# Token loops staged with lags, one product spread over the barriers, and weight transposes in 128-row pieces, in a forward-and-backward transformer block

## The chip, the cores and the metric

The kernel runs on one core of one Trainium2 chip. The metric is the device time of one execution in microseconds (us); quoted times are medians over several executions. Engines are named as in the profile: PE is TensorE (matmul), PEld its weight loads, DVE is VectorE, ACT is ScalarE, POOL is GpSimd, SP is Sync, which here only issues transfers. "SPq" lines are Sync's transfer issues. "Hole" below means a stretch in which TensorE is idle.

## The reference

One block of linear attention followed by a SwiGLU feed-forward layer, each behind a LayerNorm, and all its gradients.

```python
def A(x, wqkv, wo):                       # 2048 tokens, D = 640, 32 heads of 20
    q, k, v = split_heads(x @ wqkv)
    phi = lambda t: where(t > 0, t + 1, exp(t)) + 1e-6
    pq, pk = phi(q), phi(k)
    kv, z = sum_tokens(pk * v), sum_tokens(pk)
    o = (pq @ kv) / (pq . z + 1e-6)
    return o @ wo
def B(x, w_gate, w_up, w_down):           # F = 1728
    return (silu(x @ w_gate) * (x @ w_up)) @ w_down
h  = x + A(layernorm(x), wqkv, wo)
h2 = h + B(layernorm(h), w_gate, w_up, w_down)
# outputs: h2, and the gradients of x, wqkv, wo, w_gate, w_up, w_down for a given grad_out
```

Everything is bfloat16. Token tiles have 128 rows, so there are 16 of them.

## The kernel before

The work is a line of stages with whole-token barriers between them. The names below are used throughout.

1. k/q loop: LayerNorm, transpose of the tile (`xnT`), products for k and q; then `z`.
2. `y`, `kvt`, `w2`: three small matrix products that make `W2`, while VectorE makes `pqs`.
3. a loop: `pqs @ W2`, second LayerNorm (`hn`, with `rstd` on GpSimd), transpose `hnT`.
4. `dm`: `grad_out @ w_down^T`, 32 steps of ten matmuls.
5. gate/up block, four times: `pg`, `pu`, VectorE's derivatives, transposes `stg`, then the weight gradients `dw`.
6. dhn/dp loop; 7. `gt`, `dkvt`, `wv2`, `dz`; 8. dk/dxn loop; 9. weight gradients `dwqk`, `dwo`, and the o loop with the output.

The parts that the change and the argument touch:

```python
for t in tiles:                                        # stage 1
    ... transposes of tile t on TensorE, copy of xnT on ScalarE ...
    for (dst, w0) in ((pk, D), (pqa, 0)):              # k and q of the SAME tile
        ps = mm("ps_kq"); mm_row(ps, xnT of tile t, wqk)
    if t % 4 == 3:
        nc.gpsimd.dma_start(out=scr_xn..., ...)        # also pk, pq and four of xnT
...
nc.gpsimd.dma_start(out=mat_v(scr_W2), in_=W2[:])      # stage 2: W2 stored plain
for t in range(ST + 1):                                # stage 3, hn one tile behind
    ...
for g in range(4):                                     # stage 4: all dm in one block
    for t in range(0, ST, 2):
        ... 10 matmuls; evacuation dme; nc.gpsimd.dma_start(out=scr_dm..., in_=dme)
...
W2T = mat("W2T")
nc.sync.dma_start_transpose(out=W2T[:], in_=scr_W2)    # stage 6: whole matrix
for t in range(ST + LAG):                              # dp two tiles behind dhn
    ...
nc.sync.dma_start_transpose(out=woT[:], in_=A_wo)      # whole matrices, also wqkvT, G, KV, Y, dKV
...
for t in range(ST + LAG):                              # stage 8
    nc.gpsimd.dma_start(out=xtv, in_=scr_xnT[t])       # loads of this tile, just in time
    nc.gpsimd.dma_start(out=pkr[:], in_=scr_pk_v[:, t, :])
    nc.sync.dma_start_transpose(out=pkT, in_=pkr[:])
    ...
```

A property of the program: a scheduler orders each engine's instructions at build time, by what it expects to be ready. So an instruction's place in a queue isn't its place in the source.

Of the kernel before, what the change touches and what calls it, by code (L numbers as in the profile page):

```python
# [9 lines left out]
BF16 = mybir.dt.bfloat16  # L10
# [4 lines left out]
P = 128  # L15
# [4 lines left out]
def kernel(  # L20
# [15 lines left out]
    LAG = 2  # L36
    GW = [448, 448, 448, 384]
# [53 lines left out]
    scr_W2 = dram.tile([D, D], BF16, name="scr_W2")  # L91
# [34 lines left out]
    def ln_rstd(mv, mean, rstd, t0, nt):  # L126
        v = small.tile([P, 4], FP32, name="lnv", tag="lnv")
        nc.gpsimd.tensor_scalar(out=v[:, :nt], in0=mv[:, :nt, 1], scalar1=1e-5, scalar2=None, op0=ALU.add)
        nc.gpsimd.tensor_tensor(out=rstd[:, t0:t0 + nt], in0=v[:, :nt], in1=nhalf[:, :nt], op=ALU.pow)
# [30 lines left out]
    dm0 = strips.tile([P, ST, GM], BF16, name="dm0", tag="S")  # L160
# [3 lines left out]
    for (t0, t1) in ((0, 1), (1, 2), (2, 4)):  # L164
        nc.sync.dma_start(out=x_tm[0][:, t0:t1, :], in_=x_v[:, t0:t1, :])
    for (c0, c1) in ((D, 2 * D), (0, D)):
        nc.scalar.dma_start(out=wqk[:, :, c0:c1], in_=A_wqkv[:, c0:c1].rearrange("(k p) n -> p k n", p=P))
    for (t0, t1) in ((4, 8), (8, 12), (12, 16)):
        nc.sync.dma_start(out=x_tm[t0 // 8][:, t0 % 8:(t1 - 1) % 8 + 1, :], in_=x_v[:, t0:t1, :])
# [25 lines left out]
    wvo = strips.tile([P, 2, DT, D], BF16, name="wvo", tag="S")  # L195
# [6 lines left out]
    pqa = big.tile([P, ST, D], BF16, name="pqa", tag="B")  # L202
    for (t0, t1) in ((0, 1), (1, 2), (2, 4), (4, 6), (6, 8), (8, 10), (10, 12), (12, 14), (14, 16)):
# [4 lines left out]
        for t in range(t0, t1):  # L208
# [6 lines left out]
            for (dst, w0) in ((pk, D), (pqa, 0)):  # L215
                ps = mm("ps_kq")
                mm_row(ps, lambda k: xnT[:, k, t * P:(t + 1) * P], lambda k, n0, n1: wqk[:, k, w0 + n0:w0 + n1], DT)
                e = fw("phi_e")
                r = fw("phi_r")
                nc.scalar.activation(out=e[:, :, :320], in_=row(ps), func=ACT.Exp)  # L220
                nc.scalar.activation(out=r[:, :, :320], in_=row(ps), func=ACT.Relu)
                nc.vector.tensor_scalar(out=e[:, :, :320], in0=e[:, :, :320], scalar1=1.0, scalar2=1e-6,
                                        op0=ALU.min, op1=ALU.add)
                nc.vector.tensor_tensor(out=half(dst[:, t, :]), in0=e[:, :, :320], in1=r[:, :, :320], op=ALU.add)
            if t % 4 == 3:
                sl = slice(t - 3, t + 1)
                nc.gpsimd.dma_start(out=scr_xn_v[:, sl, :], in_=xn[:, sl, :])
                nc.gpsimd.dma_start(out=scr_pk_v[:, sl, :], in_=pk[:, sl, :])
                nc.gpsimd.dma_start(out=scr_pq_v[:, sl, :], in_=pqa[:, sl, :])
                for tt in range(t - 3, t + 1):  # L230
                    nc.gpsimd.dma_start(out=scr_xnT[tt], in_=xnT[:, :, tt * P:(tt + 1) * P])
# [5 lines left out]
    nc.gpsimd.dma_start(out=wvo[:, 0], in_=A_wqkv[:, 2 * D:3 * D].rearrange("(k p) n -> p k n", p=P))  # L237
    nc.gpsimd.dma_start(out=wvo[:, 1], in_=A_wo.rearrange("(k p) n -> p k n", p=P))
# [6 lines left out]
    for i in range(DT):  # L245
# [3 lines left out]
        nc.scalar.copy(out=mask[:, i, :e1 - e0], in_=ps[:, 0, :e1 - e0])  # L249

# [22 lines left out]
    nc.gpsimd.dma_start(out=mat_v(scr_Yt), in_=Yt)  # L273
    for j in range(DT):
# [7 lines left out]
    W2 = big.tile([P, DT, D], BF16, name="W2", tag="B")  # L282
    for i in range(DT):
# [4 lines left out]
    nc.gpsimd.dma_start(out=mat_v(scr_W2), in_=W2[:])  # L288
# [4 lines left out]
    for t in range(ST + 1):  # L293
# [355 lines left out]
```

## Time and profile before

| | kernel before |
|---|---|
| time | 1001.98 us, median of 3 (1001.32 to 1008.93) |
| profiled execution | 1011.5 us, mean granted TensorE clock 0.958 |
| TensorE busy | 859.4 us, 85% |
| TensorE idle | 152 us; the prediction below sums it by stage |

How to read it: the page first gives each engine's busy time; then 40 slices of the span, a digit being the busy share in tenths. A timeline line has start, length, engine, source line, operation, output<-inputs, shapes, number of instructions, and in brackets the idle time just before the group and what ended it. The lines themselves are in the prediction below.

### The profile page before, as it was taken

To read this page: it belongs to the slowest core of one execution; us is meant where nothing else is said; L and a number is where in the kernel's file an instruction comes from. 1 tells how busy PE (TensorE), PEld (TensorE's weight loads), DVE (VectorE), ACT (ScalarE), POOL (GpSimd) and SP (SyncE) were. 2 spreads that over 40 slices of the span, in tenths; PEclk is the share of its full clock that TensorE was granted. 3 is DMA by queue.
4 is the path that set the end of the run, shared out by engine and by line. 5 is a ranking of instruction groups with operands and counts; after the bars stand their busy time and mean duration, and the time that the engine had idled before them with its cause. 6 is when DMAs were issued, how large, how long until landed. Compare 5 with 4: busy or idle time off the path is not lost.

```text
span 1011.5 us, 14023 instructions
## 1 busy us (share of the span) xinstructions
PE 859.4 (85%) x5461; PEld 533.6 (53%) x5461; DVE 425.0 (42%) x889; ACT 299.2 (30%) x421; POOL 253.1 (25%) x430
## 2 busy tenths in 40 slices
PE   2667956999999999999999199997948777997996
PEld 1445634555455455455567177775725454674663
DVE  6733988205705704804701067777113333400111
ACT  1666110447515514614501022222201222311100
POOL 5732136442232221231242001011101212113321
PEclk9999979999999999999999699998978999998998
DMA  9993598987995992982869935137798555699521
GB/s 285 153 282 117 123 237 203 212 210 182 208 285 110 231 276 65 216 221 49 205 204 210 111 103 187 33 116 229 173 204 189 121 124 134 106 242 290 147 79 39
DMA packets 277938, 174.82 MB, mean 173 GB/s; under 512 B 236032, under 2 KB 259264, under 8 KB 277872
## 3 DMA queue, kind: packets, MB, share of 16 engines
q1 hardware_dynamic: 251312, 79.36, 43.1%
q0 software_dynamic: 25248, 92.94, 29.8%
q10 hardware_dynamic: 1312, 1.64, 0.5%
q8 instruction: 42, 0.69, 0.3%
q14 instruction: 24, 0.20, 0.1%
HBM read 52.90 MB, written 64.01 MB: 116 GB/s over the span
## 4 chain that ended last, share of the span: by engine, by line
PE 54%; DVE 15%; DMA 13%; issue 6%; SPq 5%; ACT 3%; POOL 2%; POOLq 0%; DVEq 0%; ACTq 0%
PE ps_dw L400 16%; PE ps_dhn L117 10%; PE ps_dm L321 6%; PE ps_kq L117 5%; PE ps_dxn L550 3%; PE ps_o L599 3%; DMA ring<-pkr 2%; PE ps_dp L117 2%; DMA dh1T<-dh 2%; PE ps_gt L117 2%; SPq L592 2%; DMA xt<-scr_xnT 2%; PE pg L357 2%; DVE m_s L383 1%; DVE m_s L377 1%
## 5 line engine op out<-in xcount | busy, mean ns | idle before, releaser
L400 PE MATMUL ps_dw<-dd,hn 128*128 128x448 bf16 (+1 forms) x640 | 119.9, 346 | 7.0 <-DVE dd L382 6.9
L117 PE MATMUL ps_dhn<-wgT,cols 128*128 128x320 bf16 x864 | 120.8, 301 | 0.0
L117 PEld LDWEIGHTS <-cols 128*128 128x128 bf16 x864 | 85.1, 98 | 33.8
L400 PEld LDWEIGHTS <-hn 128*128 128x128 bf16 x640 | 62.6, 98 | 62.3 <-issue 8.7
L387 POOL DMA_DIRECT2D scr_dT<-stg x64 | 34.6, 541 | 171.5 <-DMA stg<-dd 153.2
L402 DVE CAST dwev<-ps_dw 128x896 bf16<-128x896 f32 (+3 forms) x12 | 10.9, 907 | 150.4 <-PE ps_dw L400 150.4
L117 PE MATMUL ps_kq<-wqk,xnT 128*128 128x320 bf16 x320 | 48.3, 308 | 26.2 <-ACT xnT L214 26.2
L550 PEld LDWEIGHTS <-ring 128*128 128x128 bf16 x480 | 49.6, 104 | 37.4 <-DMA ring<-dk 14.8
L599 PE MATMUL ps_o<-wd,mT 128*128 128x320 bf16 x448 | 67.7, 300 | 0.0
L550 PE MATMUL ps_dxn<-wqkvT,ring 128*128 128x320 bf16 x320 | 55.8, 318 | 13.8 <-DMA ring<-dk 13.8
L362 PE MATMUL pu<-wgu,hnT 128*128 128x448 bf16 (+1 forms) x320 | 63.6, 346 | 0.0
L357 PE MATMUL pg<-wgu,hnT 128*128 128x448 bf16 (+1 forms) x320 | 63.6, 346 | 0.0
L402 ACT CAST dwev<-ps_dw 128x896 bf16<-128x896 f32 (+1 forms) x20 | 17.6, 878 | 152.1 <-PE ps_dw L400 118.8
L400 PE MATMUL ps_dw<-m_s,dh 128*128 128x448 bf16 (+1 forms) x320 | 60.4, 346 | 0.0
L601 DVE TENSOR_TENSOR h1r<-ps_o,h1r 128x640 bf16<-128x640 f32 x16 | 13.2, 824 | 110.7 <-PE ps_o L599 110.7
L321 PE MATMUL ps_dm<-wdT,dh2T 128*128 128x448 bf16 (+1 forms) x320 | 58.6, 346 | 0.8 <-DVE xr L299 0.8
L599 PEld LDWEIGHTS <-mT 128*128 128x128 bf16 x448 | 41.2, 97 | 26.4 <-issue 8.4
L117 PEld LDWEIGHTS <-xnT 128*128 128x128 bf16 x320 | 30.8, 100 | 41.3 <-ACT xnT L214 29.1
L117 PE MATMUL ps_dp<-W2T,dh1T 128*128 128x320 bf16 x160 | 26.8, 320 | 26.8 <-DMA dh1T<-dh 26.8
L117 PE MATMUL ps_dk<-wvk,xt 128*128 128x320 bf16 x160 | 28.1, 332 | 23.2 <-DMA xt<-scr_xnT 18.8
L321 PEld LDWEIGHTS <-dh2T 128*128 128x128 bf16 x320 | 31.3, 98 | 28.0 <-issue 1.0
L357 PEld LDWEIGHTS <-hnT 128*128 128x128 bf16 x320 | 31.3, 98 | 27.1
(157 smaller groups left out, 1346.9 us busy)
## 6 DMA issues: line engine op xcount, KB each, us to landing
cols<-scr_dT POOLq DMA_DIRECT2D x8, 1728.0 KB, 7.6
scr_dT<-stg POOLq DMA_DIRECT2D x48, 224.0 KB, 3.5
scr_m<-m_s POOLq DMA_DIRECT2D x12, 448.0 KB, 4.7
scr_dm<-dme POOLq DMA_DIRECT2D x16, 224.0 KB, 3.7
dm_s<-scr_dm SPq DMA_DIRECT2D x2, 1792.0 KB, 11.2
out_dram<-dwev POOLq DMA_DIRECT2D x30, 112.0 KB, 4.0
scr_dT<-stg POOLq DMA_DIRECT2D x16, 192.0 KB, 3.3
scr_xn<-xn POOLq DMA_DIRECT2D x4, 640.0 KB, 16.9
```

Source lines behind the costliest of these rows:

```text
L117: nc.tensor.matmul(ps[:, ci, :320], lhsT=lhs(k), rhs=rhs(k, n0, n1), start=(start and k == 0), stop=(stop and k == n - 1))
L321: nc.tensor.matmul(ps[:, c, :w], lhsT=dh2T[:, kt, (t + c) * P:(t + c + 1) * P], rhs=wdT[g // 2][:, kt, o:o + w], start=(kt == 0), stop=(kt ...
L357: nc.tensor.matmul(pg[:, c, :w], lhsT=hnT[:, kt, (t + c) * P:(t + c + 1) * P], rhs=wg[:, kt, 0:w], start=(kt == 0), stop=(kt == DT - 1))
L362: nc.tensor.matmul(pu[:, c, :w], lhsT=hnT[:, kt, (t + c) * P:(t + c + 1) * P], rhs=wg[:, kt, w:2 * w], start=(kt == 0), stop=(kt == DT - 1))
L377: nc.vector.tensor_tensor(out=m, in0=m, in1=dg, op=ALU.mult)
L387: nc.gpsimd.dma_start(out=scr_dT[t + c, :, KO[g]:KO[g] + GK[g], :], in_=stg[:, :GK[g], :])
L400: nc.tensor.matmul(ps[:, c, :w], lhsT=lhs(t), rhs=rhs(t), start=(t == 0), stop=(t == ST - 1))
L402: copy(out=ev[:, :len(parts), :w], in_=ps[:, :len(parts), :w])
L550: nc.tensor.matmul(ps[:, ci, :320], lhsT=lhs[:, i, :], rhs=rhs[:, i, n0:n1], start=(k == 0 and i == 0), stop=(k == 2 and i == DT - 1))
L592: nc.sync.dma_start_transpose(out=mT[:, t % 4], in_=scr_m[t * P:(t + 1) * P, :])
L599: nc.tensor.matmul(ps[:, ci, :320], lhsT=mT[:kk, t % 4, j, :], rhs=wd[:kk, j, n0:n1], start=(j == 0), stop=(j == FT - 1))
L601: nc.vector.tensor_tensor(out=half(h1r[:]), in0=row(ps), in1=half(h1r[:]), op=ALU.add)
```

## The change

The intent is to remove TensorE's idle time without touching its 5461 matmuls: delay the consumer in each token loop by one to four tiles, put dm products where TensorE waits, and break the weight transposes into pieces so that an urgent transpose needn't wait for a whole matrix. The core of the diff (cuts marked):

```diff
+    LAG_C = 4
@@ the x and wqk loads are split over Sync's and ScalarE's queues [cut] @@
@@ k/q loop: products one tile later, stores on Sync @@
-            for (dst, w0) in ((pk, D), (pqa, 0)):   [body moved into kq(t)]
-                nc.gpsimd.dma_start(out=scr_xn_v[:, sl, :], in_=xn[:, sl, :])   [and pk, pq, xnT]
+            if t > 0:
+                kq(t - 1)                            [its stores: nc.sync.dma_start]
@@ dm as a generator, called in the barriers @@
+    dm(1)            [after y]      dm(1) [after kvt]     dm(3) [after w2]
+            dm(1)    [each tile of the a loop]
+            if g == 0:
+                dm(2)   [between pg and pu of the first gate/up block]
-    for g in range(4):  [the dm block]
@@ W2: transposed by pieces at the end of the a loop @@
-    nc.gpsimd.dma_start(out=mat_v(scr_W2), in_=W2[:])
+    for i in range(DT):
+        w2t = wk("w2t")
+        nc.sync.dma_start_transpose(out=w2t..., in_=W2[:, i, :])
+        nc.gpsimd.dma_start(out=mat_v(scr_W2T)[:, :, i * P:(i + 1) * P], in_=w2t...)
-    for t in range(ST + 1):
+    for t in range(ST + 2):                          [hn two tiles behind]
@@ dw: w_down's product first, last two tiles deferred [cut] @@
@@ dhn/dp loop @@
+    def tr_mat(dst, src):
+        for i in range(DT):
+            nc.sync.dma_start_transpose(out=dst[:, :, i * P:(i + 1) * P], in_=src[i * P:(i + 1) * P, :])
-    nc.sync.dma_start_transpose(out=W2T[:], in_=scr_W2)
+    nc.sync.dma_start(out=W2T[:], in_=mat_v(scr_W2T))
-    for t in range(ST + LAG):
+    for t in range(ST + LAG_C):
@@ woT, wqkvT, G, KV, Y, dKV: tr_mat in place of one transpose each [cut] @@
@@ dk/dxn loop @@
+    xnT_r resident: four loads on GpSimd;  pk loaded two tiles ahead, transposed from DRAM
+    dwqk(0)          [in front of the loop instead of behind it]
+        if t >= ST:
+            dwqk(1, t - ST, t - ST + 1)
@@ end: dwo and dwqk outputs alternate between two pools [cut] @@
```

Left out of the cuts above: the addition in front of `rstd` moves from GpSimd to VectorE, VectorE's operations in the gate/up block change their order, and a few buffers and loads move.

One instruction isn't in the diff, since it is unchanged: the last transpose of the kernel, `dwd` (the w_down gradient, 2.3 MB), and its store `out_6` on GpSimd.

## The prediction

> **What bounds the kernel now.** I read the page first, then every idle stretch of TensorE in its timeline, then the chain of waits around the longest of them, then the Sync queue's timeline.
>
> ```profile
> PE 859.4 (85%) x5461; PEld 533.6 (53%) x5461; DVE 425.0 (42%) x889; ACT 299.2 (30%) x421; POOL 253.1 (25%) x430
> ...
> PE   2667956999999999999999199997948777997996
> ...
> PEclk9999979999999999999999699998978999998998
> ```
>
> TensorE is busy 859.4 of 1011.5 us; the other engines are under half. So the span is TensorE's work plus 152 us in which it idles, and the slices under 9 show where: the start, slices 13 to 17 in part, one hole at slice 22, and the last third. The change has the same 5461 matmuls (the built order shows it), so it can win only idle time and the matmuls that run on a slow clock after it. TensorE's timeline says what ended each idle stretch (in brackets):
>
> ```profile
> 25.45 2.89 PE L117 MATMUL ps_kq<-wqk,xnT 128*128 128x320 bf16 x20 [1.70 <-ACT xnT L214]
> ...
> 148.60 6.40 PE L117 MATMUL ps_a<-W,pqsT 128*128 128x320 bf16 x30 [9.66 <-DVE xr L299]
> ...
> 176.42 58.56 PE L321 MATMUL ps_dm<-wdT,dh2T 128*128 128x448 bf16 x320 [0.75 <-DVE xr L299]
> ...
> 271.33 7.73 PE L400 MATMUL ps_dw<-dd,hn 128*128 128x448 bf16 x40 [1.55 <-DVE dd L382]
> ...
> 577.50 2.83 PE L117 MATMUL ps_dp<-W2T,dh1T 128*128 128x320 bf16 x10 [20.41 <-DMA dh1T<-dh]
> ...
> 702.26 2.85 PE L117 MATMUL ps_dp<-W2T,dh1T 128*128 128x320 bf16 x10 [6.40 <-DMA dh1T<-dh]
> ...
> 759.04 2.85 PE L550 MATMUL ps_dxn<-wqkvT,ring 128*128 128x320 bf16 x10 [8.96 <-DMA ring<-dk]
> ...
> 803.43 1.93 PE L117 MATMUL ps_dk<-wvk,xt 128*128 128x320 bf16 x10 [2.45 <-DMA xt<-scr_xnT]
> ```
>
> Summed by stage: start 17.8; k/q loop 15 x 1.70 = 25.5; from z to the dm products 20.8; dw products 6.9; dp loop 20.4 + 6.4 = 26.8; dk/dxn loop and its entry 37.8; dwqk 7.3; after the last matmul 8.8. Together 151.7, so no idle time is unexplained. The chain of waits shows the mechanism of the two DMA-bound stages:
>
> ```profile
> 549.19 9.99 SPq L485
> ...
> 559.24 18.02 DMA dh1T<-dh
> ...
> 800.78 3.58 DMA ring<-pkr
> ...
> 807.37 0.46 POOL out_dram L554
> ...
> 807.90 3.66 DMA xt<-scr_xnT
> 811.61 1.53 PE ps_dk L117 x10
> ```
>
> The first dh1T transpose stands behind the whole-matrix W2T and woT transposes in Sync's queue and then takes 18.02 us. In the dk loop each tile runs a full circle: pk load, its transpose, VectorE, the dx store, and only then does GpSimd issue the next xt load.
>
> ```profile
> 15.13 44.10 SPq L192 DMA_TRANSPOSE dh2T<-in_grad_out_dram  x4
> 59.28 11.99 SPq L188 DMA_TRANSPOSE wdT<-in_B_w_down_dram  x3
> 104.52 39.62 SPq L263 DMA_TRANSPOSE pqsT<-pqs  x15
> ```
>
> Sync is occupied until 71 us by transposes nobody needs before 176 us; this matters below.
>
> **What the Trainium skill says.** (1) "TensorE: Matmul & The Clock Gate", Part 1: idle time lets the clock gate fall to half rate, and about 3.4 us of work lift it. The trace agrees: granted clock 0.55 between 560 and 580 us, and the dp group after the hole took 2.83 us instead of 1.52. Removing a hole wins a little more than the hole. (2) The same page, "Architectural detail": ScalarE and VectorE are strict FIFO, and matmuls keep program order. So dm fills a hole only if it stands before the waiting matmul; the built order has it there. (3) "DMA: Bandwidth & Descriptors", "Issuing engines are not separate DMA queues": moving stores from GpSimd to Sync buys no bandwidth. The DMA share of 0.99 to 1.24 in the first 60 us says the engines are full there. (4) The same page, "Latency and other measured facts", gives 261 GB/s for DMA transposes. The trace has both: 10.7 us of issue for the 2.3 MB dwd transpose alone (some 290 GB/s between 903 and 906 us), but 48 GB/s in all between 30 and 36 us, when GpSimd's copies share the engines. No page I found explains this.
>
> **The change, part by part** (profile time; durations from the timeline).
>
> *Start and k/q loop.* x tiles and weights are split over two queues. VectorE still does seven pairs of bn_stats, at 0.37 us each, before the first normalised tile. With x landing at about 5 us I expect the first k/q group near 13.7 us, against 18.51. The group of tile t-1 now follows the transposes of tile t, so the ScalarE copy is off TensorE's path: period 4.87 - 1.70 = 3.17 us. ScalarE starts an operation every 0.60 us, five per tile: 3.0. VectorE: 0.75 + 0.11 + 0.36 + four at about 0.41 = 2.9. All under 3.17, narrowly. End of z: 13.7 + 2.1 (slow clock) + 16 x 3.17 + 4.4 = 71, before 100.7.
>
> *From z to the first gate product.* TensorE's work: y 21.9, masks 0.8, kvt 2.1, w2 5.4, a 16 x 1.36 = 21.8, and 21 of the 32 dm steps at 58.56 / 32 = 1.83, which is 38.4; sum 90.4. VectorE's pqs chain is 16 x 2.72 = 43.5, and its share of the a loop 2.5 per tile, under TensorE's 1.36 + 1.83 = 3.19. The first evacuation of a waits for the end of the pqs chain, 71.5 + 43.5 + about 6 for transpose and xr load = 121. TensorE arrives with its four PSUM buffers full at about 115. I leave 7 us idle: 97.5, before 134.1 with all of dm in it.
>
> *Gate/up and dw.* The 11 other dm steps, 20.1 us, sit in the first block between pg and pu, where VectorE (7 x 0.60 = 4.2 per pair) gains time. With the dw_down product first and its last two tiles deferred, 28 matmuls x 0.189 = 5.3 us cover VectorE's tail, of which 6.9 was visible. Stage: 300.1 + 20.1 - 6.6 = 313.6.
>
> *dhn/dp.* W2T becomes a plain load, woT five pieces, lag four: dp of tile 0 is due 5 x 7.33 = 36.7 us after the start instead of 22, and its transpose no longer stands behind both matrices. The 20.4 goes. At the end dp of tile 15 needs 9.1 us after the last dhn, and only four dp groups (5.4) stand before it: 3.7 remain of 6.4. Stage: 16 x 7.33 + 11 x 1.36 + 11.3 = 143.5, before 170.
>
> *Entry and dk/dxn.* dwqk of q (21.8) moves in front of the loop and covers dzE and the WK2 transposes. Entry 33 + 21.8 = 54.8, before 33.4. In the loop xnT is resident, pk comes two tiles ahead, and its transpose reads DRAM directly, so the circle is cut. A tile costs 1.36 + 4.08 = 5.44; Sync's three issues of 1.25 and VectorE's 3.6 lie below it. 87, plus 8.7 for two dwqk pieces moved into the last rounds, plus 3 for the first dkT, which stands behind 15 pieces of G, KV and Y: 98.7, before 136.9.
>
> *Rest.* 127.5 - 21.8 - 8.7 (moved) - 7.3 (two pools of output buffers) - 1.5 (clock) = 88.2. I add 5: GpSimd's order has the dwd output, whose transpose is now last in Sync's queue, between the first and second o store. End unchanged, 8.8.
>
> **Sum:** 71 + 97.5 + 313.6 + 143.5 + 54.8 + 98.7 + 93.2 + 8.8 = 881, against 1011.5. Times the ratio of timed to profiled, 1001.98 / 1011.5, that is 873. I add 5 for waits such a sum cannot see: **878 us**.
>
> **Rivals.** *A: Sync becomes the bound of the first 170 us.* The 10.5 MB of xn, pk, pq and xnT stores now stand in Sync's queue behind all the early transposes and ahead of pqsT. If the transposes again last until 71 us, the stores end near 95 to 105, VectorE stalls after two or three pqs tiles for want of work buffers, and the gain of the k/q loop is given back: 20 to 30 us, so 900 to 908. For it: 44.10 us for dh2T. Against it: that slow stretch had GpSimd's copies beside it, and those are gone. *B: DMA mixing at the dk entry.* xn_r, 15 wqkvT pieces and the 2.6 MB xnT_r load on GpSimd meet during GT; if rates fall to 100 GB/s, WK2 or the first dkT comes 10 to 15 us late: 890. *C: the o loop blocks on GpSimd's dwd output:* up to 10 more, 883. *D: nothing resists:* no added waits, all slow-clock loss gone: 860.
>
> **Range and chances.** A at a quarter, B and C at a third each in part, D at a tenth give 858 to 908 as the range for 8 in 10. Even A and B together stay over 7% below 1002, and the sum's smallest sure parts (25.5 + 20.4 + 20) exceed the 2% threshold three times. Faster 0.98, same 0.015, slower 0.005.
>
> **What would show it.** k/q groups every 3.2 us and z over near 71; no 9.66 hole but a short one before the a loop; no wait on dd in front of dw; no 20.41 hole; dk/dxn tiles every 5.4 us with no wait on xt; TensorE idle about 35 to 45 us in all. I am wrong if Sync's first pqsT issue comes much after 75 us (A), if the dk loop waits on ring or wvk (B), or if o waits on PSUM for h1r (C).

## The result, and the profile after

The changed kernel takes **917.73 us** (four runs, 914.36 to 925.69), where the kernel before took 1004.62 us in the same rounds. The ratio is 0.914, with a 95% interval of 0.907 to 0.922. Ratios here are the mean time of one kernel's fast runs over that of the other's fast runs of the same rounds, so they are not quite the ratios of the medians. Executions over 1.5% slower than the fastest of the same kernel are left out of the means. The direction was right; 917.7 lies outside the predicted range of 858 to 908.

The page of the changed kernel: the busy time of the engines, and TensorE's busy share and granted clock in 40 slices.

```profile
PE 847.8 (93%) x5461; PEld 531.7 (58%) x5461; DVE 425.6 (46%) x914; ACT 297.8 (33%) x421; POOL 217.7 (24%) x367
...
PE   4999899769999999999999999996997999999596
...
PEclk9999999889999999999999999998999999999799
```

TensorE is busy for 848 of 916 us and idle for 68, where the prediction had said 35 to 45. The slices at 7 or less (each is 22.9 us) are the first, 8 and 9, 28, 31, 38 and the last: start and end, and the five holes below. TensorE's timeline names what ended the larger idle stretches; the first line shows an undisturbed k/q group for comparison.

```profile
36.60 2.88 PE L118 MATMUL ps_kq<-wqk,xnT 128*128 128x320 bf16 x20
...
170.38 3.89 PE L385 MATMUL pg<-wgu,hnT 128*128 128x448 bf16 x10 [5.24 <-DVE xr L337]
...
199.44 3.08 PE L271 MATMUL ps_dm<-wdT,dh2T 128*128 128x384 bf16 x10 [6.64 <-ACT m_s L405]
...
639.83 2.85 PE L118 MATMUL ps_dp<-W2T,dh1T 128*128 128x320 bf16 x10 [8.01 <-DMA dh1T<-dh]
...
710.35 2.85 PE L614 MATMUL ps_dxn<-wqkvT,ring 128*128 128x320 bf16 x10 [5.72 <-DMA ring<-dk]
...
757.99 2.42 PE L614 MATMUL ps_dxn<-wqkvT,ring 128*128 128x320 bf16 x10 [2.18 <-DMA ring<-dk]
...
859.74 48.62 PE L652 MATMUL ps_o<-wd,mT 128*128 128x320 bf16 x308 [10.76 <-ACT dwv L665]
```

The 1.70 us in front of every k/q group, the 9.66 in front of the a loop, the 20.41 in front of the first dp and all waits on `xt` are gone, as predicted. Five holes of 5 to 11 us are left. By stage (profile time; a stage ends where the next one's first product begins, so the 5.24 us in front of the first gate product count to the stage before it; only the wait in front of the first dk product, 4.34 us in the kernel before, counts to the dk/dxn loop):

| stage | before | predicted | after | missed by |
|---|---|---|---|---|
| start to end of z | 100.7 | 71 | 70.8 | -0.2 |
| z to first gate product | 134.1 | 97.5 | 99.6 | +2.1 |
| four gate/up blocks with dw | 300.1 | 313.6 | 323.5 | +9.9 |
| dhn/dp loop | 170.0 | 143.5 | 148.5 | +5.0 |
| gt to first dk product | 33.4 | 54.8 | 56.6 | +1.8 |
| dk/dxn loop | 136.9 | 98.7 | 107.9 | +9.2 |
| to the last o product ("rest") | 127.5 | 93.2 | 101.4 | +8.2 |
| tail | 8.8 | 8.8 | 7.8 | -1.0 |
| sum | 1011.5 | 881 | 916.1 | +35 |

What stands behind the holes is seen in the queues of the other engines. First GpSimd and VectorE at the end of the a loop:

```profile
165.43 0.91 POOL L355 DMA_DIRECT2D scr_W2T<-w2t  x1 [7.01 <-DMA w2t<-W]
...
168.54 0.56 POOL L130 TENSOR_TENSOR rstd<-lnv,nhalf 128x1 f32<-128x1 f32 x1
```

```profile
169.15 0.45 DVE L348 TENSOR_SCALAR hn<-xr,mv,rstd 128x640 bf16<-128x640 bf16 x1 [8.16 <-POOL rstd L130]
```

GpSimd stands for 7.01 us on the store of a transposed piece of W2, because that piece isn't there yet. The next `rstd` is behind it in the queue, VectorE waits 8.16 us for it, and the evacuation `xr` that frees TensorE's PSUM buffer is behind that. Then ScalarE, inside the first gate/up block:

```profile
190.16 0.80 ACT L277 CAST dme<-ps_dm 128x768 bf16<-128x768 f32 x1 [5.12 <-DMA scr_dm<-dme]
197.67 0.92 ACT L404 ACTIVATE nsg<-pg 128x896 bf16<-128x896 f32 x1 [6.72 <-DMA scr_dm<-dme]
```

The evacuated dm products and the scratch tiles of the block share six buffers; ScalarE waits twice until a dm store has landed. Sync's queue, for the stages from dp on (start, time from first to last issue of the group):

```profile
631.02 1.21 SPq L496 DMA_TRANSPOSE dh1T<-dh  x1
632.28 0.62 SPq L525 DMA_DIRECT2D xn_r<-scr_xn  x1
632.95 34.99 SPq L470 DMA_TRANSPOSE wqkvT<-in_A_wqkv_dram  x15
...
686.66 6.53 SPq L470 DMA_TRANSPOSE G<-scr_GT  x5
693.24 6.57 SPq L470 DMA_TRANSPOSE KV<-scr_KVT  x5
699.99 7.04 SPq L470 DMA_TRANSPOSE Y<-scr_Yt  x5
707.13 3.86 SPq L603 DMA_TRANSPOSE ring<-dk  x3
```

The last dh1T transpose is issued at 631.02 and TensorE resumes at 639.83, so it took 8.8 us, with 2.6 MB loads of `pqs_tm` and `xn_r` beside it. The first dk transpose is issued at 707.13, right behind 20.1 us of G, KV and Y. And GpSimd in the o loop:

```profile
849.61 1.15 POOL L670 DMA_DIRECT2D out_dram<-dwd  x1 [19.83 <-DMA dwd<-scr_dwdT]
850.75 1.12 POOL L655 DMA_DIRECT2D out_dram<-h1r  x2
```

The store of the w_down gradient waits 19.83 us for its transpose, and the o stores behind it (`h1r`) hold the buffers that the `dwv` evacuations need, on which TensorE waits.

### The profile page after: what moved, and what is told of

Same layout as the page of the kernel before. It is cut to its first block, busy times and chain, and to the rows that moved or that the text cites. A ratio compares the mean times of both kernels' runs of the same rounds, so it can differ in the third digit from the quotient of the medians.

```text
span 916.1 us, 14047 instructions
## 1 busy us (share of the span) xinstructions
PE 847.8 (93%) x5461; PEld 531.7 (58%) x5461; DVE 425.6 (46%) x914; ACT 297.8 (33%) x421; POOL 217.7 (24%) x367
## 5 line engine op out<-in xcount | busy, mean ns | idle before, releaser
L652 PE MATMUL ps_o<-wd,mT 128*128 128x320 bf16 x448 | 69.8, 306 | 10.8 <-ACT dwv L665 10.8
L271 PE MATMUL ps_dm<-wdT,dh2T 128*128 128x448 bf16 (+1 forms) x320 | 65.5, 357 | 8.4 <-ACT m_s L405 6.6
L385 PE MATMUL pg<-wgu,hnT 128*128 128x448 bf16 (+1 forms) x320 | 65.5, 353 | 5.2 <-DVE xr L337 5.2
L614 PE MATMUL ps_dxn<-wqkvT,ring 128*128 128x320 bf16 x320 | 53.7, 309 | 8.1 <-DMA ring<-dk 8.1
L385 PEld LDWEIGHTS <-hnT 128*128 128x128 bf16 x320 | 31.7, 99 | 33.6 <-issue 7.3
L439 PEld LDWEIGHTS <-dh 128*128 128x128 bf16 x320 | 31.3, 98 | 28.0 <-issue 1.0
L392 PEld LDWEIGHTS <-hnT 128*128 128x128 bf16 x320 | 31.3, 98 | 26.8
L407 DVE TENSOR_TENSOR m_s<-m_s,dd 128x896 bf16<-128x896 bf16 (+1 forms) x32 | 19.3, 604 | 54.1 <-ACT m_s L405 54.1
```

The costliest lines, as they stand in the source:

```text
L271: nc.tensor.matmul(ps[:, c, :w], lhsT=dh2T[:, kt, (t + c) * P:(t + c + 1) * P], rhs=wdT[g // 2][:, kt, o:o + w], start=(kt == 0), stop=(kt ...
L385: nc.tensor.matmul(pg[:, c, :w], lhsT=hnT[:, kt, (t + c) * P:(t + c + 1) * P], rhs=wg[:, kt, 0:w], start=(kt == 0), stop=(kt == DT - 1))
L392: nc.tensor.matmul(pu[:, c, :w], lhsT=hnT[:, kt, (t + c) * P:(t + c + 1) * P], rhs=wg[:, kt, w:2 * w], start=(kt == 0), stop=(kt == DT - 1))
L407: nc.vector.tensor_tensor(out=m, in0=m, in1=dg, op=ALU.mult)
L439: nc.tensor.matmul(ps[:, c, :w], lhsT=lhs(t), rhs=rhs(t), start=(t == 0), stop=(t == ST - 1))
L614: nc.tensor.matmul(ps[:, ci, :320], lhsT=lhs[:, i, :], rhs=rhs[:, i, n0:n1], start=(k == 0 and i == 0), stop=(k == 2 and i == DT - 1))
```

## The experiments

Eighteen kernels ran; all were correct. The kernel before ran in the rounds of each call (its medians were 1003 to 1006 us), so kernels of different calls are compared by their ratios to it. Each edit is to the changed kernel unless another is named. The times below are medians. One thing to keep in mind: stages that an edit doesn't touch still vary between profiled runs by a few us. In six kernels with W2, dm and the first block as in the changed kernel, the four blocks took 323.5, 324.5, 324.9, 324.9, 325.6 and 327.9 us, and the larger hole of the first block was between 5.60 and 10.89 us. Likewise, in the fast profiles that leave the place as the change has it, the dp tail hole was 5.4 to 8.3 us, the dk/dxn loop took 104.4 to 110.2 us, and the hole of the o loop was 7.5 to 13.3 us. A profile is also one run: that of experiment 4 (903.33 us) was 7 us and that of `mends_and_late_loads` (882.71) 9 us below its kernel's median.

### 1. The out_6 store on another queue

```diff
-    nc.gpsimd.dma_start(out=out_6[0:13 * P, :]..., in_=dwd[:, :13, :])     [and the last 64 rows]
+    nc.sync.dma_start(out=out_6[0:13 * P, :]..., in_=dwd[:, :13, :])
```

> The changed kernel, with the two stores of the w_down gradient (out_6) issued by the Sync engine, which also issues the transpose they wait for, in place of GpSimd. Theory: the 10.76 us hole of TensorE in the o loop exists only because these stores stand in GpSimd's queue between the first and the second store of o and wait 19.83 us for the transpose. Then the hole goes (under 2 us left), the last stage falls from 101.6 to about 91 us, nothing before it moves, and the time is 906 to 909 us against 917.7. Rival: the hole is a bandwidth matter, the 2.3 MB transpose and the wd and scr_m transfers share the DMA engines, and the o stores would land late from any queue. Then at least 6 us of idle time stay in the o loop and the time stays above 913 us.

Measured: 906.73 us, ratio 0.902. TensorE's timeline of this kernel in the o loop:

```profile
847.91 50.72 PE L652 MATMUL ps_o<-wd,mT 128*128 128x320 bf16 x336
```

There is no bracket left: the hole is gone, and the last stage took 88.5 us. The o stores were late because of their place in a queue; the transfers that they share the DMA engines with are the same.

### 2. W2 stored plain

```diff
-    for i in range(DT):  [five transposes of W2 on Sync and five stores on GpSimd, end of the a loop]
+    nc.gpsimd.dma_start(out=mat_v(scr_W2T), in_=W2[:])        [right after w2, untransposed]
-    nc.sync.dma_start(out=W2T[:], in_=mat_v(scr_W2T))
+    tr_mat(W2T, scr_W2T)                                      [stage 6]
```

> The changed kernel, with W2 stored plain after its product and transposed in five pieces at the start of the dhn stage, instead of transposed and stored at the end of the a loop. Theory: the 5.24 us hole in front of the first gate product comes from the five stores of the transposed pieces, which stand in GpSimd's queue ahead of the last rstd operations and wait for Sync's transposes; with them gone the hole is under 1.5 us, the first gate product begins near 165.5 instead of 170.4 us. At the start of the dhn stage the five transposes return to Sync, but with lag four the first dp product is not due for some 37 us, so nothing is lost there (no hole above 1 us in front of the first dp). Time 911 to 914 us. Rival: the a loop is held by the load and transpose traffic itself (slow xr loads and hnT transposes), so the hole stays above 4 us, or the dp hole of the kernel before (20.41 us) comes back because five transposes stand ahead of the first dh1T, which would make it 930 us or more.

Measured: 900.29 us, ratio 0.895. One of the four runs (909.55) was slow; the median of the three fast ones is 897.99. That is three to five times the gain that I had expected. TensorE's and GpSimd's timelines of this kernel:

```profile
165.55 2.06 PE L271 MATMUL ps_dm<-wdT,dh2T 128*128 128x448 bf16 x10
167.44 2.05 PE L382 MATMUL pg<-wgu,hnT 128*128 128x448 bf16 x10
...
200.83 1.78 PE L271 MATMUL ps_dm<-wdT,dh2T 128*128 128x384 bf16 x10 [0.77 <-ACT m_s L402]
```

```profile
166.64 0.56 POOL L130 TENSOR_TENSOR rstd<-lnv,nhalf 128x1 f32<-128x1 f32 x1 [0.57 <-DVE lnv L129]
```

The hole in front of `pg` is gone, and so, which I hadn't expected, are the two in the first gate/up block: the four blocks took 313.4 us, against 313.6 predicted for the change. No wait appeared in front of the first dp. So nearly all of the first 12 us of the miss come from ten instructions, the five transposes and five stores of W2.

### 3. The same stores on Sync: queue or transfers?

```diff
-        nc.gpsimd.dma_start(out=mat_v(scr_W2T)[:, :, i * P:(i + 1) * P], in_=w2t...)
+        nc.sync.dma_start(out=mat_v(scr_W2T)[:, :, i * P:(i + 1) * P], in_=w2t...)
```

> The changed kernel, W2 still transposed at the end of the a loop, but its five stores issued by Sync instead of GpSimd. This takes apart what storing W2 plain had removed. Theory A: the harm was GpSimd's queue, where the stores waited for the transposes ahead of the last rstd operations. GpSimd is now free, rstd comes in time, and the 5.24 and 8.19 us holes fall as they did with the plain store (first gate product at 166 to 168 us, first block to the end of its last dw stage 313 to 315 us in all). Theory B: the harm was the five transposes and five stores themselves, in Sync's queue and on the DMA engines next to the hnT transposes and GpSimd's loads of dh2. Sync now waits for its own transposes too, so the last hnT is later still: first gate product at 172 us or later, and the first-block hole stays above 6 us.

Measured: 911.48 us, ratio 0.909. TensorE, GpSimd and ScalarE:

```profile
166.28 2.06 PE L385 MATMUL pg<-wgu,hnT 128*128 128x448 bf16 x10
...
211.91 3.35 PE L271 MATMUL ps_dm<-wdT,dh2T 128*128 128x384 bf16 x10 [13.02 <-ACT m_s L405]
```

```profile
202.81 0.57 POOL L417 DMA_DIRECT2D scr_dT<-stg  x1 [21.49 <-DMA stg<-dd]
...
206.63 1.45 POOL L278 DMA_DIRECT2D scr_dm<-dme  x2 [1.17 <-issue]
```

```profile
210.15 0.92 ACT L404 ACTIVATE nsg<-pg 128x896 bf16<-128x896 f32 x1 [15.83 <-DMA scr_dm<-dme]
```

Each theory is right about one hole. The one in front of `pg` was GpSimd's queue: it is gone. The one in the first block is larger than before (13.02 us), and its chain can be read here: Sync is late with W2, so the first `stg` transpose lands late; GpSimd stands 21.49 us on its store; the dm stores behind it are issued at 206.63; ScalarE gets its buffer at 210.15. Moving the waiting stores between queues moved the wait.

### 4. Order alone: weight transposes behind the block's own

```diff
-                nc.sync.dma_start_transpose(out=stg...)
+                last_stg = nc.sync.dma_start_transpose(out=stg...)
...
+            behind(tr, last_stg)     [each wgT transpose is issued after this block's last stg]
```

> The changed kernel, with one order edit in Sync's queue: the transposes of a block's gate/up weights (wgT), needed only in the dhn stage, are issued behind that block's own sixteen stg transposes instead of wherever the scheduler put them (the first five stand ahead of the first stg). Theory: the hole of 6.64 us in the first block is a chain: Sync is late by the W2 and wgT transposes (19.38 us for four), the first stg transpose lands late, GpSimd stands on its store and the dm stores behind it, the buffers of dm evacuations stay taken, ScalarE and TensorE wait. With wgT out of the way stg comes some 15 us earlier, the hole falls under 2 us, and the time is 909 to 913 us; the 5.24 us hole before the block stays. Rival: the DMA engines are the limit there, so dm stores land late in any order and the hole stays at 5 us or more; time 916 us or more.

Measured: 910.34 us, ratio 0.906. GpSimd, ScalarE and TensorE:

```profile
182.03 1.43 POOL L282 DMA_DIRECT2D scr_dm<-dme  x2
```

```profile
192.00 0.92 ACT L408 ACTIVATE nsg<-pg 128x896 bf16<-128x896 f32 x1 [6.34 <-DMA scr_dm<-dme]
```

```profile
193.76 3.36 PE L275 MATMUL ps_dm<-wdT,dh2T 128*128 128x384 bf16 x10 [3.73 <-ACT m_s L409]
```

The time is as the theory said, the hole only half: 3.73 us stay, and the four blocks took 318.6 us. Order in Sync's queue is one part. The other is that transfers land slowly there: the dm store for whose buffer ScalarE waits was issued at 182.03 us and landed 9.9 us later, where such a store took 3.7 us in the median of the kernel before. Four loads of `dh` had been issued just ahead of it, and the DMA share was 0.97 to 1.08 between 170 and 190 us. Which transfers slow it isn't isolated.

### 5. All dm in the a loop

```diff
-            dm(1)
+            dm(1 if t < 5 else 2)
-            if g == 0:
-                dm(2)
```

> The changed kernel, with two dm steps instead of one in each of the last eleven tiles of the a loop, so that none is left for the first gate/up block. Theory: the two holes of the first block (1.55 and 6.64 us) come from dm evacuations that wait for buffers which slow dm stores hold, while transposes and GpSimd copies share the DMA engines there. With no dm in it the holes go; the block is then bound by VectorE (4.2 us a pair against 3.8 of TensorE), which gives 2 to 3 us back; the a loop grows by the 20.1 us of the moved products. Sum: first gate product near 190, end of the first block's eight pairs at or a little before the changed kernel's, time 911 to 915 us. Rival: the stores are slow because so many transfers are in flight, wherever they stand: the same waits on dm stores then appear at the end of the a loop with 4 to 8 us, and the time stays at 917 to 921 us.

Measured: 915.22 us, ratio 0.910, which can't be told from the changed kernel's 0.914. From z to the first dhn product it took 427.5 us against 423.1. The holes of the first block did go, but waits of 3.0 us came at the end of the a loop, and others of 1.5 to 3.1 us around the dw products. Inconclusive on its own; it fits that the transfers of this stretch, not the place of the dm products, hold things up.

### 6. dm in one block, with W2 transposed early and with W2 plain

```diff
-    dm(1) ... dm(1) ... dm(3) ... dm(1) per tile ... dm(2) per pair
+    dm(99)                                  [once, after the a loop]
```

> The changed kernel, with all 32 dm steps in one block after the a loop, as before, everything else kept. Theory: dm in the barriers fills the waits of TensorE on VectorE's pqs chain and on the a evacuations. Without it the wait before the first a product comes back with about 10 us and the a loop waits 1.7 us on some tiles, while the holes of the changed kernel at the end of the a loop and in the first gate/up block (5.24 + 8.19 us) go, because the block of 58.6 us gives the queues time to drain. z to the end of the first gate/up block's products: about 5 to 10 us more than the changed kernel at most: 918 to 928 us. Rival: the filling is worth its full 20 us (all waits between z and dm of the kernel before): 935 us or more.

> The kernel with W2 stored plain (900.3 us), and all 32 dm steps in one block after the a loop as before. With W2 transposed at the end of the a loop the block had cost nothing (920.0 against 917.7), though it brought the 9.0 us hole in front of the first a product back. Theory: the placement of dm in the barriers is worth 10 to 15 us, but the W2 transposes had taken that back; the block version didn't pay for them in the same place. With W2 plain the block then shows its full cost: z to first dhn 418 to 424 us against 408.1, and 911 to 917 us. Rival: the placement is worth nothing by itself, since the a loop with dm runs at the same sum; then the time is 899 to 904 us.

Measured: 919.96 us, ratio 0.914, on the changed kernel; 922.21 us, ratio 0.919, on the kernel with W2 plain (900.29, 0.895). TensorE's timeline in the first of the two:

```profile
119.63 7.61 PE L118 MATMUL ps_a<-W,pqsT 128*128 128x320 bf16 x40 [9.01 <-DVE xr L334]
...
184.96 26.12 PE L271 MATMUL ps_dm<-wdT,dh2T 128*128 128x448 bf16 x140 [4.82 <-ACT dme L277]
```

The old hole of 9 us in front of the a loop is back. Yet with W2 transposed early, spreading dm over the barriers is worth nothing in the time, and with W2 plain it is worth 22 us (24 by the ratios). From z to the first dhn product: 423.1 and 431.9 us with W2 early (spread, block), 408.1 and 429.2 with W2 plain. The spread placement needs GpSimd and the transfers to keep pace, and the W2 pieces took that away; the block waited elsewhere anyway. The first time lies in its expected range; the second lies above it, since I had put the placement at 10 to 15 us.

### 7. Lag of dp: two tiles instead of four

```diff
-    LAG_C = 4
+    LAG_C = 2
```

> The changed kernel, with the dp products two tiles behind dhn instead of four. Theory: the 20.41 us hole came from the first dh1T standing behind two whole-matrix transposes in Sync's queue and landing late; the plain load of W2T and the five woT pieces remove most of that, and at lag two the first dp product is due 22 us after the start of the stage. A hole of 3 to 8 us comes back there, and the tail hole at the last dp grows, as only two dp groups (2.7 us) stand in front of it: 8.0 becomes 10.7. Time 923 to 930 us. Rival: the lag alone removed the hole, so all 20 us come back: 936 us or more. Second rival: the queue alone did it and the lag is not needed: 915 to 920 us.

> The kernel with W2 stored plain and transposed in pieces in the dhn stage (900.3 us), and the dp products two tiles behind dhn instead of four. With W2 transposed early, lag two had cost nothing (917.5 against 917.7). Theory: lag four and the early transpose are two remedies for one wait, either alone is enough. Without both, the first dh1T stands behind ten pieces again, dp of tile 0 is due 22 us after the start of the stage, and a hole of 8 to 20 us comes back: 909 to 920 us. Rival: five-piece transposes let dh1T pass early, so neither remedy is needed: no hole above 2 us, 899 to 903 us.

Measured: 917.48 us, ratio 0.912, on the changed kernel: the second rival is right and the lag of four alone is worth nothing. With W2 plain it is another matter: 913.53 us, ratio 0.913, against 0.895 at lag four. TensorE's timeline there:

```profile
508.86 1.79 PE L118 MATMUL ps_dp<-W2T,dh1T 128*128 128x320 bf16 x10 [4.12 <-DMA dh1T<-dh]
```

The dhn/dp loop took 154.9 us instead of 146.9. The rest of the 13 us (18 by the ratios) lies in stages that the edit doesn't touch, so the size beyond 8 us isn't shown. Lag four and the early transpose of W2 are two remedies for one wait. The change has both, and the early transpose is the one with a price.

### 8. Whole-matrix transposes again

```diff
-        for i in range(DT):
-            nc.sync.dma_start_transpose(out=dst[:, :, i * P:(i + 1) * P], in_=src[i * P:(i + 1) * P, :])
+        nc.sync.dma_start_transpose(out=dst, in_=src)
```

> The changed kernel, with every transpose of a weight-sized matrix (woT, the three of wqkvT, G, KV, Y, dKV) issued whole, as in the kernel before, in place of five pieces each. Theory: the pieces are the dearer form; 15 of them took 34.99 us of Sync's issue where three whole ones had taken 18.58, and the 15 of G, KV and Y stand ahead of the first dkT. Whole, Sync reaches the first dkT about 7 us earlier (20.1 less 12.5), the 5.72 us entry hole goes, and the time is 910 to 914 us. Rival: the pieces were the point of the change, because a short transpose lets the urgent ones pass; whole ones then hold up the last dh1T, WK2 or dkT by 4 us each, the holes at the dp tail and the dk entry grow to 10 us and more, and the time is 922 to 930 us.

Measured: 912.82 us, ratio 0.909. By the time alone that isn't safely apart from 0.914; the stage tells it. Sync and TensorE:

```profile
684.11 4.20 SPq L469 DMA_TRANSPOSE G<-scr_GT  x1
688.36 3.71 SPq L469 DMA_TRANSPOSE KV<-scr_KVT  x1
692.24 4.25 SPq L469 DMA_TRANSPOSE Y<-scr_Yt  x1
703.07 4.39 SPq L602 DMA_TRANSPOSE ring<-dk  x3
```

```profile
707.74 2.85 PE L613 MATMUL ps_dxn<-wqkvT,ring 128*128 128x320 bf16 x10 [2.07 <-DMA ring<-dk]
```

G, KV and Y occupy Sync for 12.2 us instead of 20.1 and are done before the first dk is ready. The dk/dxn loop took 100.1 us instead of 107.9. So the pieces, the part of the change that was to let urgent transposes pass, cost 8 us there against the changed kernel's own profile (4 to 10 against the 104.4 to 110.2 of all kernels with pieces), and no wait in this profile grew for want of them.

### 9. G, KV and Y into the loop

```diff
-    tr_mat(G, scr_GT)      [and KV, Y]
+    tr_mat(G, scr_GT, dk_tr[3])      [issued behind the 4th dk transpose; KV the 7th, Y the 10th]
```

> The changed kernel, with the issue order of Sync changed only: the pieces of G, KV and Y go behind the fourth, seventh and tenth dk transpose instead of ahead of the first. Theory: the 5.72 us hole at the entry of the dk/dxn loop is Sync's queue, since 15 pieces (20.1 us of issue) stand ahead of the first dkT, which was ready about 5 us earlier. Then the hole falls under 1.5 us and the time is 911 to 914 us, if the pieces fit between the loop's own transposes (per tile 3 x 1.3 of 5.4 us used, 5 pieces need 6.6 us). Rival: Sync has no room in the loop, so the same 5 us come back as waits on the ring in three later tiles; the loop keeps 106 to 108 us and the time is unchanged within 2 us.

Measured: 923.15 us, ratio 0.920. TensorE's timeline:

```profile
708.25 2.85 PE L621 MATMUL ps_dxn<-wqkvT,ring 128*128 128x320 bf16 x10 [2.99 <-DMA ring<-dk]
...
752.06 2.75 PE L621 MATMUL ps_dxn<-wqkvT,ring 128*128 128x320 bf16 x10 [4.15 <-DMA ring<-dk]
...
761.76 2.23 PE L621 MATMUL ps_dxn<-wqkvT,ring 128*128 128x320 bf16 x10 [2.42 <-DMA ring<-dk]
...
777.19 1.53 PE L621 MATMUL ps_dxn<-wqkvT,ring 128*128 128x320 bf16 x10 [2.72 <-DMA ring<-dk]
```

The rival is right, and more: the entry hole halves, but the loop gets three waits (4.15, 2.42 and 2.72 us) for one of 2.18, and took 113.6 us. Sync has no room for pieces inside this loop.

### 10. Without the k/q lag, and the k/q stores back on GpSimd

```diff
-            if t > 0:
-                kq(t - 1)
+            kq(t)
```

> The changed kernel, with the k/q products of a tile right behind its own transposes again, as before. Theory: this lag is the whole gain of the k/q loop: the wait of 1.70 us per tile on the copy of xnT comes back 15 or 16 times, the period goes from 3.00 to 4.87 us, and the end of z moves from 70.7 to about 99 us. Since VectorE, ScalarE and Sync all trail TensorE here, little is caught up later: 940 to 946 us. Rival: the stage is bound by the DMA share (near 1 in the first 60 us) or by VectorE (2.9 us a tile); the change of store queue is what helped, and the period stays under 3.6 us: the time stays below 928 us.

Measured: 947.97 us, ratio 0.942. The mechanism is the one expected, the time 2 us above the range. Start to z took 98.9 us against 70.8, with the period back at 4.87 us. This lag is worth 28 us, the largest single term, and the later stages caught up no more of it than their scatter (the profiled span is 25 us longer, the time 30).

```diff
-            nc.sync.dma_start(out=scr_xn_v[:, sl, :], in_=xn[:, sl, :])     [and pk, pq, xnT]
+            nc.gpsimd.dma_start(out=scr_xn_v[:, sl, :], in_=xn[:, sl, :])
```

> The changed kernel, with the stores of xn, pk, pq and xnT in the k/q loop on GpSimd's queue again, as before. Theory: transposes on Sync run slowly next to GpSimd's copies, 44 us for dh2T in the kernel before against 21 us here; back on GpSimd, they fill Sync until 60 us or more again. TensorE's k/q loop needs none of them, and pqsT's first issue, due at 75 us, still finds Sync free: time within 3 us, 914 to 921 us, with dh2T's issue at 30 us or more. Rival: the k/q loop depends on it: stores on GpSimd hold up rstd (GpSimd computes it) and the loop's period rises to over 3.3 us, 923 us or more.

Measured: two fast runs, 939.98 and 933.76 us, ratio 0.934; two more runs (949.55 and 967.61) were slow, and the profiled one was one of those. Its sizes are therefore only indicative; the order of things is not. Sync in the changed kernel for comparison, then Sync, VectorE and TensorE of this run:

```profile
13.40 21.06 SPq L197 DMA_TRANSPOSE dh2T<-in_grad_out_dram  x4
```

```profile
13.41 72.49 SPq L197 DMA_TRANSPOSE dh2T<-in_grad_out_dram  x4
...
107.00 35.80 SPq L299 DMA_TRANSPOSE pqsT<-pqs  x15
```

```profile
110.25 0.82 DVE L297 TENSOR_TENSOR pqs<-pqa,rall 128x640 bf16<-128x640 bf16 x1 [22.06 <-DMA pqsT<-pqs]
```

```profile
128.27 0.74 PE L315 MATMUL ps_kvt<-yk,wvo 128*128 128x140 bf16 x5 [24.86 <-DVE yk L317]
```

The time is the rival's, the mechanism neither's: the k/q stage itself ended only 6.2 us later (77.0 against 70.8). The early dh2T transposes took 72.49 us instead of 21.06, Sync reached pqsT at 107 instead of 75, VectorE stalled for want of a buffer, and TensorE with it. From the late transposes on this is the chain of the predicted Rival A, though with the stores in the other queue. The change avoids it because Sync issues these stores only behind the early transposes, from 41.76 us on. Whether it matters that GpSimd issued them, or only that they ran beside the transposes, isn't separated.

### 11. The mends together

`three_mends` is experiments 1, 2 and 8 in one kernel.

> Three edits together in the changed kernel: W2 stored plain, matrices transposed whole, out_6 stored from Sync. Alone they gave 17.4, 4.9 and 11.0 us of the median. Theory: they act on holes in different stages (end of the a loop and first block; dk loop; o loop) and add up: about 33 us, 882 to 888 us; the stages are z to dhn 408, dk/dxn 100, rest 88 to 90. Rival: with W2 and woT whole again at the start of the dhn stage and with the DMA engines busier per us, a hole comes back in front of the first dp or in the o loop; then 892 us or more.

Measured: 887.91 us, ratio 0.885. The expected range holds, at its upper edge. z to first dhn 412.1, dk/dxn 101.0, rest 88.5.

`mends_and_late_loads` adds an order at the end of the dp loop:

```diff
-    nc.sync.dma_start(out=pqs_tm[:], in_=scr_pqs_v)
+    for c in range(4):
+        ld = nc.sync.dma_start(out=pqs_tm[:, 4 * c:4 * c + 4], in_=scr_pqs_v[:, 4 * c:4 * c + 4])
+        behind(ld, last_dh1T)
...
+        behind(ld, gt_store)          [the xnT_r loads, in GpSimd's queue]
```

> The three mends (887.9 us), and the order of loads at the end of the dhn/dp stage changed: pqs_tm comes in four parts behind the last dh1T transpose, and the xnT_r load waits in GpSimd's queue behind the store of G. Theory: the wait of 6.4 us in front of the last dp product is half made of dh1T's landing in the company of 7.8 MB of loads; alone it lands in about 4 us instead of 8 to 9, and the hole falls to 2 to 3.5 us. pqs_tm then comes later, so part of it may come back as waits in the first GT product. Together 884 to 886 us. Rival: the hole is the chain from the last dhn product over VectorE and the transpose, about 6 us whatever the load; it stays above 5 us and the late loads of pqs_tm cost 3 to 8 us more: 888 to 896 us.

Measured: 891.94 us, ratio 0.887. TensorE's timeline:

```profile
620.24 1.53 PE L118 MATMUL ps_dp<-W2T,dh1T 128*128 128x320 bf16 x10 [2.25 <-DMA dh1T<-dh]
...
689.80 2.85 PE L617 MATMUL ps_dxn<-wqkvT,ring 128*128 128x320 bf16 x10 [5.84 <-DMA ring<-dk]
```

The theory about the dp tail holds: without the loads beside it the last dh1T lets TensorE wait 2.25 us, and the dhn/dp loop took 143.1 us, where 143.5 had been predicted. But the loads have to run at some time, and the dk entry pays: 5.84 us instead of 2.11, loop 108.7 us instead of 101.0. The net is nothing. `all_mends` (with experiment 4 added) shows the same:

> The three mends (887.9 us), the late loads, and wgT behind stg in every block. Theory: the holes of the first block (5.5 us left with the three mends) and of the dp tail (6.4, to 3) go together, for they lie in different stages: 878 to 883 us, about what had been predicted for the change itself. Rival: the W2T and wqkvT transposes and loads that are moved back meet others, and the sum stays at 885 us or more.

Measured: 886.93 us, ratio 0.883, with 9.83 us at the dk entry. The expected sum failed.

Last, G, KV and Y whole and behind the loop's last dk transpose, with the k weight gradient's last pieces ahead of the w_o gradient to cover them, and the first two pk loads ahead of xnT_r; without and with the late loads:

```diff
+    tr_mat(G, scr_GT, dk_tr)          [dk_tr: the last dk transpose; also KV, Y]
+    dwqk(1, 2)                        [ahead of dwo instead of behind it]
+    load_pk(0); load_pk(1)            [ahead of the xnT_r loads]
+        behind(mt_tr, dkv_tr)         [mT from tile 6 on behind dKV; dwd behind the last mT]
```

> The three mends and wgT behind stg; and the whole-matrix transposes of G, KV and Y behind the last dk transpose in Sync's queue, so that none stands in the dk/dxn loop or ahead of it; the k weight gradient's last three pieces (13 us of TensorE) ahead of the w_o gradient to cover them; the first two pk loads ahead of the xnT_r load; loads of pqs_tm and xnT_r as in the changed kernel. Theory: the entry hole (2.1 us with the three mends, 9.8 with all mends) is Sync's queue; it goes below 1 us, the loop takes 97 to 99 us against 101 to 110, and the time is 877 to 882 us. Rival: G and KV now come too late for the w_o gradient or mT too late for the o loop, and 4 us or more come back there: 885 us or more.

> The same, with the late loads of pqs_tm and xnT_r in addition. Theory: with nothing of G, KV and Y at the loop's entry, the 3.5 us that the late loads won at the dp tail are kept: dhn/dp 143.5, loop 97 to 100, 874 to 879 us. Rival: the late xnT_r load is itself in the way of the first dk and WK2 transposes; the entry hole stays at 4 us or more and the time is that of the other run or above, 880 us or more.

Measured: 886.52 us, ratio 0.882, without the late loads; 880.04 us, ratio 0.877 (0.874 to 0.880), with them. The first missed its range: its entry hole is still 2.35 us, and a wait of 3.80 us for wqkvT appeared ahead of `wv2`. The second is one us above its range. The late loads, which brought nothing before, are worth about 6 us now that the dk entry has room; the two intervals still touch, so that size is a likely one only. The page of the last kernel (of the fastest of its six runs, 874.54 us):

```profile
PE 836.0 (96%) x5461; PEld 527.3 (60%) x5461; DVE 425.9 (49%) x914; ACT 297.7 (34%) x421; POOL 212.5 (24%) x361
...
PE   4999899989999999999999999999799999999997
...
PEclk9999999999999999999999999999999999999999
```

It is 4% faster than the changed kernel (0.877 over 0.914), TensorE is idle for 37 us of 872.8, and the clock row has no dip left: TensorE's busy time fell by 12 us with the same matmuls.

## Why the prediction was wrong, point by point

**Right: the gain of the lags.** z over at 70.8 us (71 predicted); the k/q period measured 3.00 us where nothing disturbed it, a little under the 3.17 predicted. Without the lag 28 us come back, 25.5 had been claimed. The 20.41 us of the first dp are gone. The waits on `xt` are gone.

**Right about what was ruled out.** Rival A did not happen (first pqsT issue at 75.10). The reason given, that GpSimd's copies are no longer beside the transposes, is what the store queue experiment shows: with them back, Sync is late and the stall comes. Rival B's sign did appear, waits on `ring` in the dk/dxn loop, but from Sync's queue (experiment 8) and not from slow rates at the dk entry. Rival C came true.

**Wrong: z to dhn, +12 us.** The failed step is an omission, a wait that has no place in the sum. The prediction priced "W2T becomes a plain load" in the dhn stage and never priced where the transposes and stores had gone. Five transposes in Sync's queue and five waiting stores in GpSimd's, at the end of the a loop, made the holes of 5.24 and 6.64 us. With W2 plain, z to dhn took 408.1 us, against 97.5 + 313.6 = 411.1 predicted, so the rest of the working for these stages was close. That the first of the two stages alone came out at 99.6 for 97.5 is luck: the 7 us of idle time allowed in front of the a loop did not come (TensorE has no wait there), and the unforeseen 5.24 us took their place.

**Wrong: the dp tail, +5.** "3.7 remain of 6.4" took dh1T's landing from the kernel before, where it was 4.5 us. It landed after 8.8 us in the company of the loads; with the loads held back the stage took 143.1 (143.5 predicted).

**Wrong: the dk/dxn loop, +9.2.** "Plus 3 for the first dkT, which stands behind 15 pieces" named the queue and mis-sized it. The pieces take 20.1 us where whole matrices take 12.2; with whole matrices the loop took 100.1 (98.7 predicted). I had not asked what five issues cost against one, though the kernel before showed the whole form at the same place: G, KV and Y took 12.5 us of issue, from 743.59 to 756.28, right ahead of its first dk transpose.

**Wrong: the o loop, +8.2.** Rival C was named with "up to 10 more" and charged with 5. It was the whole 10.76 us (7.5 to 13.3 in the other kernels), and the built order made the wait certain: the store stood between the first and second o store, and its transpose was last in Sync's queue. With the store elsewhere the rest took 88.5, and the prediction without its 5 was 88.2.

**Wrong: the scale.** The sum of 881 was multiplied by 1001.98 / 1011.5, which took off 8.3 us. But the profiled execution of the kernel before took 1013.2 us itself, longer than any of the three timed ones, and the changed kernel's profile (916.1) is as long as its times (917.7). The 5 us of margin hid part of it.

**Slips in the working.** The slices under 9 are 1 to 4, 6, 7, 23, 28, 30 to 34, 37 and 40; slices 13 to 17 are full, and the prediction's "slice 22" is the 23rd. In its point (2), the program order of matmuls stands under "The mechanism" in Part 3 of "TensorE: Matmul & The Clock Gate", not under "Architectural detail". In its point (4), 261 GB/s is the figure of "DMA: Bandwidth & Descriptors" for a non-contiguous middle dimension; for the contiguous case the same row gives about 350 to 400. The 290 and 48 GB/s are what all DMA engines moved in those windows; dwd's 2.3 MB in 10.7 us of issue are some 214 GB/s.

**What isn't settled.** In the first block queue order accounts for about half of the hole (experiment 4). That the other half is slow transfers is read from one dm store (9.9 us to landing); what slows them isn't isolated. That the late loads pay only once G, KV and Y are out of the dk entry is read from where the waits went; no run isolates it.

## What to carry to other kernels

When a change moves a wait, look up what each in-order queue will hold at the new place, and price the waiting instruction's neighbours: here ten small transfers, five of them stores ahead of GpSimd's `rstd`, undid nearly all that spreading dm had brought. A store that waits for a transfer doesn't belong in the queue of an engine that others wait for; in another queue it helps only if nothing urgent stands behind it there (experiments 1 and 3). A mend's gain may show only once the next stage has room for what was pushed into it, as with the late loads here, so test mends together as well as alone.

## What the Trainium skill lacked or had wrong

- "DMA: Bandwidth & Descriptors", "Rules for kernel authors", says "A transpose next to ordinary DMAs needs nothing". As a rule of correctness no run here contradicts it, but the time is another thing, and no page I found has it. The same four dh2T transposes took 21.06 us of issue with the stores on Sync, behind them, and 72.49 with the stores on GpSimd, beside them (a slow run; 44.10 in the kernel before).
- The same page, "Issuing engines are not separate DMA queues", says that issuing from several engines saves only the issue time. No run here contradicts it on bandwidth. What it lacks is that the queue also sets when a transfer runs: moving 10.5 MB of stores from Sync's queue to GpSimd's cost 2% of the whole time (ratio 0.934 against 0.914), since they then ran beside the early transposes, and pqsT behind those started 32 us later.
- No page I found compares a whole-matrix transpose with pieces of 128 rows: three 640 x 640 matrices took 12.2 us of issue whole and 20.1 us in 15 pieces.
